# Routed attention and a SoLU feed-forward on one core: 1024-wide steps on h, one-hot rows placed by DMA, a first pair in halves, and a new order

## The chip, the cores and the metric

The kernel runs on one core of one Trainium2 chip. The metric is the device time of an execution in microseconds (us). TensorE is called PE (PEld: its weight loads), VectorE DVE, ScalarE ACT, GpSimd POOL, and SyncE, whose queue issues nearly all transfers, SP.

## The reference

For batch 4, 8 heads, 768 tokens and 64 dimensions, each token's q and k is assigned to the nearest of 16 centroids of its head, and attention runs only between tokens of the same cluster. The result, as 3072 rows of 512, goes through a feed-forward layer with a SoLU and a layer norm.

```python
q_assign = argmax(einsum(q_n, c_n)); k_assign = argmax(einsum(k_n, c_n))
mask = q_assign[:, :, :, None] == k_assign[:, :, None, :]
scores = where(mask, q @ k.T / sqrt(D), -1e9)
x = (softmax(scores) @ v).transpose(0, 2, 1, 3).reshape(B * S, H * D)
h = x @ w_in                        # 3072 x 1024
e = exp(h - max(h))
solu = h * e / sum(e)
ln = (solu - mean(solu)) / sqrt(var(solu) + 1e-6) * g_ln
out = ln @ w_out
```

## The kernel before, in words

**Attention.** Work goes by pairs of heads, 16 pairs over four batches. A pair's q and k arrive as raw tiles by DMA and are turned to dimensions by tokens (`xt`): in batch 0 by PE transposes into PSUM and a copy (L303, L311, L313), later by a DVE transpose of 32x32 blocks (L326). The result is cast to bf16 into `qbig` and `kbig`, one of six slots (L332 to L336, on POOL or ACT). `clusters` (L346) multiplies by the centroids; DVE turns the scores back (L353), takes the maximum of 16 (L358), compares (L362, the one-hot), and turns that again (L368, `oht`). `place` (L375) copies the one-hot rows into the same tile as the vectors: rows 64 to 95 for the even head, rows 0 to 31 for the odd one, whose vector lies in rows 64 to 127. That takes eight copies of 32x192 words a pair, on POOL or DVE. Half of the 32 rows belong to the other head, and `blank` (L379) clears those of k. A score matmul (L458) over vector and one-hot rows together so gives q.k plus a large constant for equal clusters, which the exponential (L463) turns into the mask. One bank is 128x512 scores; the score ring has three banks, the ring of exponentials `e` nine. Six matmuls of 65 columns (L475) then give the values with the sum, and `normalise` (L487, L498) divides.

**Feed-forward.** There are 24 blocks f of 128 tokens. x is turned by a DMA transpose (L506); `f_h` (L539) makes h in two halves of 512, each in a bank of a ring of three; `f_max` (L546) takes a maximum of each half and `f_neg` (L550) joins them; `f_exp` (L557) and `f_u` (L563) run on each half; u is turned by a DMA transpose (L568); statistics (L574, L578) give the scale `alpha` on POOL (L584 to L590); `f_y` (L600) and `f_scale` (L606 ACT, L608 DVE) end the block, and `f_out` (L613) writes it. The last x and the last two u are turned by PE instead (L515, L525). w_in is cast by POOL (L408), w_out is scaled and centred by DVE (L425 to L437).

**The order.** Every step is put into a list by `add` with an engine, a cost, a key, and what it needs. `Weave.run` (L76) goes through the list as a planner would, with those costs, and issues each engine's instructions in the order that results. Steps that could start at about the same time go by key; FEED, PAIR and KIND shift the keys, and AWAY names the steps that go to another engine than their usual one. The order is therefore fixed when the program is built, and each engine, SP's queue too, works through its own list strictly in turn.

Of the kernel before, what the change touches and what calls it, by code (L numbers as in the profile page):

```python
# [21 lines left out]
class Weave:  # L22

    FEED_KINDS = "tx ptx tu ptu hm h ng ex u bn ag al y sc ou".split()
    PAIR_KINDS = "ld tp xa xt ca lv cv cl tb mx oh ot pl bl".split()
    FEED = [-1, 2, 2.5, 4.5, 5, 4, 6.5, 11, 18, 7.5, 8, 12.5, 7.5, 21, 10, 15.5, 16.5, 10.5,
        4.5, 7.5, 1.5, 0.5, 2.5, -0.5]
    PAIR = [-27, 0, 1.5, -6, -9, -4.5, 0, -3, 19.5, -7.5, 1.5, -3, 21, 13.5, 21, 19.5]  # L30
    KIND = {'cv': -23.5, 'wi': -36.0, 'tb': -12.0, 'ca': 16.0, 'xa': 20.0, 'N': -1.0, 'tp':
        38.0, 'lg': 36.5, 'lo': -4.0, 'pl': -3.0, 'bl': 11.5, 'z': 35.5, 'xt': -1.0, 'lv': 1.5,
        'ce': -1.0, 'oh': -1.0, 'su': 0.5, 'ld': 5.0, 'li': 4.0, 'ot': -1.0, 'cl': 0.5, 'mx':
        0.5}
    AWAY = {}
    AWAY.update(dict.fromkeys("""
        ca0.0.1.0 ca0.0.1.1 ca0.1.0.0 ca1.1.1.0 ca1.2.1.0 ca1.3.0.1 ca2.1.0.0 ca2.1.0.1
        ca2.2.0.1 ca2.3.0.0 ca3.3.0.1 xa0.0.0 xa0.2.0 xa0.2.1 xt0.2.0 xt0.2.1 xt0.3.1
    """.split(), "ACT"))
    AWAY.update(dict.fromkeys("""  # L40
        bl3.2 bl3.3 pl0.0.0.1.0 pl0.0.0.1.1 pl0.0.1.1.0 pl3.0.0.1.1 pl3.2.0.0.0 pl3.2.0.1.0
        pl3.3.0.1.0 sc15 sc17 sc22
    """.split(), "DVE"))
    AWAY.update(dict.fromkeys("""
        bl0.0 ca0.0.0.0 ca0.0.0.1 pl0.0.0.0.0 pl0.0.0.0.1 pl0.0.1.0.0 pl0.0.1.0.1
        pl0.2.1.0.1 pl0.2.1.1.1
# [4 lines left out]
    AHEAD = 2  # L51
# [5 lines left out]
    def add(self, name, eng, cost, key, fn, needs=(), after=(), take=None, give=None, move=0.0,  # L57
            bulk=False, lag=(0.5, 0.6)):
        assert name not in self.by, name
        key += self.later(name)  # L60
        self.by[name] = len(self.ops)
        self.ops.append(dict(name=name, eng=eng, cost=cost, key=key, fn=fn, needs=list(needs),
                             after=list(after), take=take, give=give, move=move,
                             bulk=bulk, lag=lag))

    def later(self, name):

        kind, rest = re.fullmatch(r"([A-Za-z]+)(.*)", name).groups()
        if kind in self.FEED_KINDS:
            return self.FEED[int(rest.split(".")[0])]  # L70
        if kind in self.PAIR_KINDS:
            b, p = rest.split(".")[:2]
            return self.PAIR[4 * int(b) + int(p)] + self.KIND.get(kind, 0)
        return self.KIND.get(kind, 0)

    def run(self):  # L76
# [67 lines left out]
        for i in order:  # L144
            ops[i]["fn"]()
# [3 lines left out]
def kernel(  # L149
# [20 lines left out]
    HALF = S // 2  # L170
    d_model = H * D
# [22 lines left out]
    ps_h = ctx.enter_context(tc.tile_pool(name="ps_h", bufs=3, space=bass.MemoryType.PSUM))  # L194
# [7 lines left out]
    def on(name, engine):  # L202
        return wv.AWAY.get(name, engine)

    R = 6
    qbig = [big.tile([P, 2, S], BF16, name=f"qbig{i}") for i in range(R)]
    kbig = [big.tile([P, 2, S], BF16, name=f"kbig{i}") for i in range(R)]
    v1 = [big.tile([P, 2, n_t, VS], BF16, name=f"v1_{i}") for i in range(R)]

    def slot(b, p):  # L210
        return (b * n_pair + p) % R

    def behind(b, p, what):
# [6 lines left out]
        return [f"{what}{n}.{k}" for n in ns for k in range(n_k if what == "S" else 2)]  # L220

    SRC, DST = (q, k), (qbig, kbig)

    def rows(h):
        return slice(0, D) if h % 2 == 0 else slice(D, P)

    def hot_rows(hh):
        return slice(D, D + NB) if hh == 0 else slice(0, NB)

    def used(h):  # L230
        return slice(0, D + NC_) if h % 2 == 0 else slice(0, P)

    n_first = 2
    UNITS, GROUPS = [], []
    for b in range(B):
        if b < B - 1:
            for p in range(n_pair):
                a, c = 2 * p, 2 * p + 1  # L240
                if p < n_pair - 1:
                    hs = [[(h, s2) for s2 in range(n_t // 2)] for h in (a, c)]
                else:
                    hs = [[(a, s2), (c, s2)] for s2 in range(n_t // 2)]
                for grp in hs:
                    GROUPS.append([])
                    for h, s2 in grp:
                        GROUPS[-1].append(len(UNITS))
                        UNITS.append((b, ((h, 2 * s2), (h, 2 * s2 + 1))))
        else:  # L250
            for h in range(2 * n_first):
                GROUPS.append([])
                for s2 in range(n_t // 2):
                    GROUPS[-1].append(len(UNITS))
                    UNITS.append((b, ((h, 2 * s2), (h, 2 * s2 + 1))))
            for su in range(n_t):
                for h in range(2 * n_first, H, 2):
                    if h % 4 == 0 or h == 2 * n_first:
                        GROUPS.append([])
                    GROUPS[-1].append(len(UNITS))  # L260
                    UNITS.append((b, ((h, su), (h + 1, su))))
    n_units = len(UNITS)
    n_k = 3
    group_of = {n: g for g, ns in enumerate(GROUPS) for n in ns}
    where = {(b, h, su): n for n, (b, subs) in enumerate(UNITS) for h, su in subs}

    def same_head(n):
        return UNITS[n][1][0][0] == UNITS[n][1][1][0]

    def spot(n, j, kt):  # L270

        if same_head(n):
            return kt // 2, (kt % 2) * 2 * P + j * P
        m = j * n_t + kt
        return m // 4, (m % 4) * P

    def first_of(b, p):
        return 2 * min(n for (b2, h, su), n in where.items() if b2 == b and h // 2 == p)
# [9 lines left out]

    def tokens(b, p, i):
        return raws[b, p, i][:].rearrange("p j c -> p (j c)").rearrange("p (t e) -> p t e", t=n_t)  # L290

    def load_tokens(b, p, i, hh, eng):
        if hh == 0:
            raws[b, p, i] = ld.tile([P, n_j, NB], F32, name="raw")
        eng.dma_start(out=tokens(b, p, i)[:, :, hh * D:(hh + 1) * D],
                      in_=SRC[i][b, 2 * p + hh].rearrange("(p t) d -> p t d" if i else
                                                          "(t p) d -> p t d", p=P))

    def turn_tokens(b, p, i, hf):

        tps[b, p, i, hf] = ps_h.tile([P, HALF], F32, name="tps", tag="hps")
        for t in range(n_t // 2):
            nc.tensor.transpose(tps[b, p, i, hf][:, t * P:(t + 1) * P],  # L303
                                tokens(b, p, i)[:, hf * (n_t // 2) + t, :], ident_f[:])

    def keep_tokens(b, p, i, hf, e):
        if hf == 0:
            xts[b, p, i] = xtp.tile([P, S], F32, name="xt")
        dst, src = xts[b, p, i][:, hf * HALF:(hf + 1) * HALF], tps[b, p, i, hf][:]
# [18 lines left out]
    def cast(b, p, i, hh, on_act=False):  # L328
        xt, h = xts[b, p, i], 2 * p + hh
        r, dst = rows(h), DST[i][slot(b, p)]  # L330
        if on_act:
            nc.scalar.activation(dst[r, hh, :], xt[r], Act.Copy, scale=inv_C if i else 1.0)  # L332
        elif i == 0:
            nc.gpsimd.tensor_copy(dst[r, hh, :], xt[r])  # L334
        else:
            nc.gpsimd.tensor_scalar(dst[r, hh, :], xt[r], scalar1=inv_C, scalar2=1.0,  # L336
                                    op0=Alu.mult, op1=Alu.mult)

    n_a = n_j // 2 * 2

    def clusters(b, p):

        csc = ps_m.tile([P, HALF], F32, name="csc", tag="m")
        for c in range(4):
            i, hf = divmod(c, 2)
            nc.tensor.matmul(csc[c * NB:(c + 1) * NB, :], c_bd[:, p, :],  # L346
                             xts[b, p, i][:, hf * HALF:(hf + 1) * HALF],
                             tile_position=(0, c * NB))
        asg[b, p, "csc"] = csc

    def turn_back(b, p):
        asg[b, p, "cst"] = pr.tile([P, n_a, NC_], F32, name="cst")
        nc.vector.transpose(asg[b, p, "cst"][:].rearrange("p a c -> p (a c)"),  # L353
                            asg[b, p, "csc"][:])

    def assign_max(b, p):
        asg[b, p, "mx"] = pr.tile([P, n_a], F32, name="mx")
        nc.vector.reduce_max(asg[b, p, "mx"][:], asg[b, p, "cst"][:], axis=AX)  # L358

    def assign_hot(b, p):  # L360
        asg[b, p, "oh"] = pr.tile([P, n_a, NC_], BF16, name="oh")
        nc.vector.tensor_tensor(asg[b, p, "oh"][:], asg[b, p, "cst"][:],  # L362
                                asg[b, p, "mx"][:].unsqueeze(2).to_broadcast([P, n_a, NC_]),
                                op=Alu.is_ge)

    def assign_turn(b, p):
        asg[b, p, "oht"] = pr.tile([P, HALF], BF16, name="oht")
# [585 lines left out]
```

## Time and profile before

| | |
|---|---|
| Median of 3 runs | 245.14 us (244.53 to 246.28) |
| Span of the profiled execution | 241.7 us |
| Instructions | 6735 |
| PE first score matmul | at 14.11 us |
| PE first feed-forward matmul | at 59.58 us |
| PE last matmul ends | at about 237.9 us |
| POOL copies of one-hot rows (L375) | 107, 39.5 us together |
| Exponentials of scores (L463) | 288, 149.5 us together |

The page gives one profiled execution: each engine's busy time, the chain of work that ended last, and groups of instructions by line with their count, busy time and the mean of one in nanoseconds. An answer by stretches gives the engines' busy times between two points of the span. The timeline lists instructions in order of time: start, length, engine, line. The runs' median lies 3.4 us above the profiled span.

### The profile page before, as it was taken

The numbers are of one execution on the slowest core, as the hardware profiler recorded it, in microseconds if no ns is written. First come the engines' busy times: TensorE is split into PE (matmuls) and PEld (weight loads), VectorE is DVE, ScalarE is ACT, GpSimd is POOL, SyncE is SP. The second block draws the span as 40 slices with busy tenths as digits, with TensorE's granted clock in tenths as the row PEclk, the third lists the DMA queues.
The fourth block names the chain that finished last, engine by engine and source line by source line (L and its number), as shares of the span: only waits on it lengthen the run. The fifth ranks groups of instructions, "written<-read, shape, count | busy, mean of one in ns | idle before, by whom it ended". The sixth has DMA issues, their size and how long they took to land.

```text
span 241.7 us, 6735 instructions
## 1 busy us (share of the span) xinstructions
PE 221.2 (92%) x2384; PEld 148.5 (61%) x2384; DVE 207.1 (86%) x427; ACT 205.4 (85%) x428; POOL 141.2 (58%) x304
## 2 busy tenths in 40 slices
PE   0969999999999999899699999999989999999983
PEld 0656675666656667666377677567657676747441
DVE  4367599999999998999699999988969779999991
ACT  2559998999788999999699999988989998969561
POOL 4973687997083485998757738888812510310331
PEclk9979999999999999999999999999999999999999
DMA  7999889797489799999799999783533444657422
GB/s 200 269 280 263 180 305 237 150 152 171 84 177 193 152 190 201 205 146 193 112 173 209 209 155 161 169 238 87 66 75 59 69 110 110 69 152 151 92 87 87
DMA packets 133217, 38.61 MB, mean 160 GB/s; under 512 B 124472, under 2 KB 128576, under 8 KB 133184
## 3 DMA queue, kind: packets, MB, share of 16 engines
q1 hardware_dynamic: 131616, 37.80, 76.9%
q10 hardware_dynamic: 1568, 0.39, 0.7%
q8 instruction: 18, 0.29, 0.5%
q14 instruction: 15, 0.12, 0.2%
HBM read 23.11 MB, written 6.29 MB: 122 GB/s over the span
## 4 chain that ended last, share of the span: by engine, by line
PE 65%; DVE 10%; DMA 7%; POOL 6%; ACT 5%; issue 5%; ACTq 0%; DVEq 0%; SPq 0%; POOLq 0%
PE sps L458 18%; PE yps L600 14%; PE hps L539 14%; PE ops L475 11%; PE csc L346 4%; ACT e L463 4%; DMA uT<-u 4%; PE tps L303 2%; DMA xT<-x 2%; DVE w_out_c L437 2%; POOL kbig L336 1%; DVE hm L546 1%; POOL qbig L334 1%; DVE qbig L375 1%; ACT e_sb L557 1%
## 5 line engine op out<-in xcount | busy, mean ns | idle before, releaser
L463 ACT ACTIVATE e<-sps 128x512 bf16<-128x512 f32 x288 | 149.5, 625 | 13.5 <-PE sps L458 12.6
L458 PE MATMUL sps<-qbig,kbig 80*128 80x256 bf16 (+3 forms) x648 | 102.2, 265 | 5.2 <-POOL qbig L375 2.1
L458 PEld LDWEIGHTS <-kbig 80*128 80x128 bf16 (+1 forms) x648 | 58.9, 122 | 24.3 <-issue 9.7
L475 PEld LDWEIGHTS <-e 128*128 128x128 bf16 x1152 | 57.5, 98 | 20.5 <-issue 3.8
L475 PE MATMUL ops<-v,e 128*128 128x65 bf16 x1152 | 65.7, 194 | 0.9 <-DVE x L498 0.6
L539 PE MATMUL hps<-w_in_sb,xT 128*128 128x512 bf16 x192 | 53.2, 379 | 2.8 <-DMA xT<-x 2.1
L600 PE MATMUL yps<-w_out_c,uT 128*128 128x512 bf16 x184 | 45.4, 379 | 1.6 <-DMA uT<-u 1.4
L557 ACT ACTIVATE e_sb<-hps,nmax 128x512 bf16<-128x512 f32 x48 | 32.9, 699 | 3.0 <-DVE nmax L550 2.9
L546 DVE TENSOR_REDUCE hm<-hps 128x1 f32<-128x512 f32 x48 | 31.9, 676 | 3.3 <-PE hps L539 2.9
L563 DVE TENSOR_TENSOR u<-e_sb,hps 128x512 bf16<-128x512 bf16 x48 | 31.6, 678 | 2.6 <-ACT e_sb L557 2.5
L375 POOL COPY kbig<-oht 32x192 f32<-32x192 f32 x57 | 20.8, 364 | 20.9 <-DVE oht L368 18.6
L574 DVE BATCH_NORM_STATS2 bs<-u 128x6 f32<-128x512 bf16 x48 | 31.6, 678 | 0.0
L600 PEld LDWEIGHTS <-uT 128*128 128x128 bf16 x192 | 17.8, 98 | 18.3 <-DMA uT<-u 1.8
L587 POOL TENSOR_SCALAR esq<-es,mv 128x1 f32<-128x1 f32 x24 | 8.2, 340 | 34.6 <-DVE mv L578 33.3
L334 POOL CAST qbig<-xt 64x768 bf16<-64x768 f32 x25 | 21.5, 859 | 6.8 <-ACT xt L311 5.9
L336 POOL TENSOR_SCALAR kbig<-xt 64x768 bf16<-64x768 f32 x28 | 23.3, 834 | 2.8 <-DVE xt L313 1.3
L539 PEld LDWEIGHTS <-xT 128*128 128x128 bf16 x192 | 17.1, 97 | 11.7 <-DMA xT<-x 2.3
L326 DVE STREAM_TRANSPOSE xt<-raw 128x768 f32<-128x768 f32 x24 | 22.1, 951 | 0.1
L375 POOL COPY qbig<-oht 32x192 f32<-32x192 f32 x50 | 18.7, 375 | 2.6
L498 DVE TENSOR_TENSOR x<-ops,den 128x384 bf16<-128x384 f32 (+1 forms) x37 | 18.6, 504 | 1.3
L389 POOL CAST v<-vf 128x384 bf16<-128x384 f32 x32 | 15.7, 514 | 6.3 <-DMA vf<-in_v_dram 3.3
L606 ACT ACTIVATE y<-yps,alpha 128x512 f32<-128x512 f32 x20 | 13.9, 694 | 5.5 <-POOL alpha L590 2.8
(74 smaller groups left out, 188.8 us busy)
## 6 DMA issues: line engine op xcount, KB each, us to landing
vf<-in_v_dram SPq DMA_DIRECT2D x16, 384.0 KB, 4.2
out_dram<-y SPq DMA_DIRECT2D x24, 256.0 KB, 2.4
raw<-in_q_dram SPq DMA_DIRECT2D x48, 96.0 KB, 3.5
raw<-in_k_dram SPq DMA_DIRECT2D x48, 96.0 KB, 2.7
w_st<-in_moe_w_in_dram SPq DMA_DIRECT2D x4, 512.0 KB, 5.6
w_g<-in_moe_w_out_dram SPq DMA_DIRECT2D x4, 512.0 KB, 7.2
raw<-in_q_dram SPq DMA_DIRECT2D x7, 192.0 KB, 4.2
raw<-in_k_dram SPq DMA_DIRECT2D x7, 192.0 KB, 4.4
```

The lines of the kernel that those rows point to most:

```text
L334: nc.gpsimd.tensor_copy(dst[r, hh, :], xt[r])
L336: nc.gpsimd.tensor_scalar(dst[r, hh, :], xt[r], scalar1=inv_C, scalar2=1.0, op0=Alu.mult, op1=Alu.mult)
L375: (nc.vector if e == "DVE" else nc.gpsimd).tensor_copy(dst, src)
L458: nc.tensor.matmul(sps_[n, k][:, c0:c0 + w], kbig[z][u, h % 2, keys], qbig[z][u, h % 2, q0:q0 + w])
L463: nc.scalar.activation(es[n, k][:], sps_[n, k][:], Act.Exp, scale=exp_scale, bias=-exp_scale)
L475: nc.tensor.matmul(opss[g][:, s, :VW], es[n, k][:, c0:c0 + P], v1[slot(b, h // 2)][:, h % 2, kt, :VW], start=(kt == 0), stop=(kt == n_t - 1))
L539: nc.tensor.matmul(ff[f, "h", f2][:], xTs[f][:, dc, :], w_in_sb[:, dc, f2 * FF2:(f2 + 1) * FF2], start=(dc == 0), stop=(dc == n_dc - 1))
L546: nc.vector.tensor_reduce(ff[f, "hm"][:, f2:f2 + 1], ff[f, "h", f2][:], axis=AX, op=Alu.max)
L557: nc.scalar.activation(ff[f, "e"][:, f2, :], ff[f, "h", f2][:], Act.Exp, bias=ff[f, "nmax"][:], accum_out=ff[f, "esum"][:, f2:f2 + 1])
L563: nc.vector.tensor_tensor(ff[f, "u"][:, f2, :], ff[f, "e"][:, f2, :], ff[f, "h", f2][:], op=Alu.mult)
L574: nc.vector.bn_stats(ff[f, "bs"][:, f2, :], ff[f, "u"][:, f2, :])
L600: nc.tensor.matmul(ff[f, "y"][:], ff[f, "uT"][:, fc, :], w_out_c[:, fc, :], start=(fc == 0), stop=(fc == n_fc - 1))
```

## The change

- The maximum of h, the exponential and the product each run once over both halves (1024 wide). h lies in a fixed region of three banks, and a block uses banks 0 and 1 or banks 1 and 2 in turn. The joining of two maxima goes; the sum of the exponentials is one number, whose scaled epsilon is formed in a step of its own.
- q and k of both heads lie in one tile `qk`; each head's vector is in rows 0 to 63 and its one-hot rows below, in rows 64 to 95. A pair is placed by four DMAs on SP's queue, which write both heads' copy at once (L437), instead of eight copies. The score matmuls of the odd head run over 96 rows, not 128.
- From the third pair on, the one-hot is made by a subtraction on POOL and a compare with zero on DVE or POOL.
- The first pair is loaded, turned, assigned and placed in two halves, by POOL copies; its score banks are 384 wide (24 of them, for 18 of 512).
- In batch 0 q is read with six tokens in a row for each partition, as k was, and the output rows are written to suit.
- Casts of q, k, v and w_in, the last copies and the scalings of y may now run on DVE too. FEED, PAIR, KIND, AWAY and many costs are new, and with them the whole order. By the built programs DVE has 18 casts of q and k (two of them of half size), 8 of v, 2 of w_in and 10 scalings of y (3 before); ACT has 15 casts (11 before) and 14 scalings (21 before).

The diff, cut to its core:

```diff
-    qbig = [big.tile([P, 2, S], BF16, name=f"qbig{i}") for i in range(R)]
-    kbig = [big.tile([P, 2, S], BF16, name=f"kbig{i}") for i in range(R)]
+    qk = [big.tile([P, 2, 2, S], BF16, name=f"qk{i}") for i in range(R)]
+    hreg = ps_h.tile([P, 3, FF2], F32, name="hreg")
...
+        else:
+            subs = [(h, 3 * s + j) for j in range(3)]
+            banks = [[(h, kt, 3 * s, 3 * P, 0)] for kt in range(n_t)]
...
+        dst = qk[slot(b, p)][:D, hh, i, cols]
...
+    def assign_less(b, p, hf):
+        nc.gpsimd.tensor_tensor(by_group(b, p, hf, "cst"), by_group(b, p, hf, "cst"),
+                                spread_max(b, p, hf), op=Alu.subtract)
...
+        if less:
+            VEC[e].tensor_scalar(asg[b, p, hf, "oh"][:, :n], asg[b, p, hf, "cst"][:, :n],
+                                 scalar1=0.0, scalar2=None, op0=Alu.is_ge)
...
-        dst = DST[i][slot(b, p)][hot_rows(hh), hh, hf * HALF:(hf + 1) * HALF].bitcast(F32)
-        (nc.vector if e == "DVE" else nc.gpsimd).tensor_copy(dst, src)
+        dst = qk[slot(b, p)][D:D + NB, :, i, lo:lo + n]
+        src = asg[b, p, hf, "oht"][r, :n]
+        if e == "SP":
+            nc.sync.dma_start(out=dst, in_=src.unsqueeze(1).to_broadcast([NB, 2, n]))
...
+    def at(f, f2):
+        return (f2, f2) if f % 2 == 0 else (1 - f2, 2 - f2)
+    def pair_of(f):
+        return hreg[:, 0:2, :] if f % 2 == 0 else hreg[:, 1:3, :]
...
-        nc.vector.tensor_reduce(ff[f, "hm"][:, f2:f2 + 1], ff[f, "h", f2][:], axis=AX, op=Alu.max)
+        nc.vector.tensor_reduce(ff[f, "nmax"][:], pair_of(f), axis=AXY, op=Alu.max, negate=True)
...
-        nc.scalar.activation(ff[f, "e"][:, f2, :], ff[f, "h", f2][:], Act.Exp,
-                             bias=ff[f, "nmax"][:], accum_out=ff[f, "esum"][:, f2:f2 + 1])
+        nc.scalar.activation(ff[f, "e"][:], pair_of(f), Act.Exp, bias=ff[f, "nmax"][:],
+                             accum_out=ff[f, "esum"][:])
...
-        nc.vector.tensor_tensor(ff[f, "u"][:, f2, :], ff[f, "e"][:, f2, :], ff[f, "h", f2][:],
-                                op=Alu.mult)
+        nc.vector.tensor_tensor(ff[f, "u"][:], ff[f, "e"][:], pair_of(f), op=Alu.mult)
...
-    for i in range(2):
-        for hh in range(2):
-            load_tokens(0, 0, i, hh, (nc.scalar, nc.sync)[hh])
+    for hf in range(2):
+        for i in range(2):
+            for hh in range(2):
+                load_tokens(0, 0, i, hh, 3 * hf, 3 * hf + 3, (nc.scalar, nc.sync)[hh])
...
+            less = idx >= 2
...
+                e = ("DVE", "POOL")[j % 2] if half else "SP"
...
+                    was = f - 1 if f2 else f - 2
+                    if was >= 0:
+                        nd.append(f"u{was}")
```

More of the change, by code (lines that the diff above doesn't have):

```diff
@@ new lines, with wide @@
+    n_units = len(UNITS)
+    group_of = {n: g for g, ns in enumerate(GROUPS) for n in ns}
+    where = {(u["b"], h, su): n for n, u in enumerate(UNITS) for h, su in u["subs"]}
+    spots = {}
+    for n, u in enumerate(UNITS):
+        for j, bank in enumerate(u["banks"]):
+            for h, kt, s0, w, c0 in bank:
+                for s in range(w // P):
+                    spots[n, h, s0 + s, kt] = (j, c0 + s * P)
+    def wide(n, j):
+        return sum(w for _, _, _, w, _ in UNITS[n]["banks"][j])
@@ L213, in behind, with first_of @@
+    time_of, spent = {}, 0
+    for n, j in BANKS:
+        time_of[n, j] = spent / (1.5 * FF2) * 2
+        spent += wide(n, j) / 2
+    t_of = [min(time_of[n, j] for j in range(len(UNITS[n]["banks"]))) for n in range(n_units)]
+    t_to = [max(time_of[n, j] for j in range(len(UNITS[n]["banks"]))) for n in range(n_units)]
+    t_all = spent / (1.5 * FF2) * 2
+    def first_of(b, p):
+        return min(t_of[n] for (b2, h, su), n in where.items() if b2 == b and h // 2 == p)
     def behind(b, p, what):
@@ L219, in behind @@
         ns = sorted({where[b0, 2 * p0 + hh, su] for hh in range(2) for su in range(n_t)})
[L220 to L278, printed above, removed]
+        return [f"{what}{n}.{j}" for n in ns
+                for j in range(len(UNITS[n]["banks" if what == "S" else "subs"]))]
     pairs = [(b, p) for b in range(B) for p in range(n_pair)]
@@ L377, in blank, with turn_back, by_group @@
-    def blank(b, p, e):
-        (nc.vector if e == "DVE" else nc.gpsimd).memset(
-            kbig[slot(b, p)][:NC_, 1, :].bitcast(F32), 0.0)
+        asg[b, p, hf, "csc"] = csc
+        asg[b, p, hf, "n"] = n
+    def turn_back(b, p, hf):
+        n = asg[b, p, hf, "n"]
+        asg[b, p, hf, "cst"] = pr.tile([P, HALF], F32, name="cst")
+        nc.vector.transpose(asg[b, p, hf, "cst"][:, :n], asg[b, p, hf, "csc"][:, :n])
+    def by_group(b, p, hf, what):
+        n = asg[b, p, hf, "n"]
+        return asg[b, p, hf, what][:, :n].rearrange("p (a c) -> p a c", c=NC_)
@@ L634 @@
     nc.vector.memset(c_bd[:], 0.0)
-    for i in range(2):
-        nc.vector.memset(DST[i][0][NB:D, 1, :].bitcast(F32), 0.0)
     nc.gpsimd.memset(v1[0][:, :, :, D:], 1.0)
@@ new lines @@
+            nd += [f"V{n0}.{j}" for j, (h, su) in enumerate(UNITS[n0]["subs"])
+                   if any(spots[n0, h, su, kt][0] == k0 for kt in range(n_t))]
+        add(f"E{n}.{k}", "ACT", 0.05 + wide(n, k) / 1200, t0 - 1,
+            (lambda e, n=n, k=k: expo(n, k)), nd, ["E{}.{}".format(*BANKS[i - 1])] if i else [])
+    prev = None
+    for g, ns in enumerate(GROUPS):
+        for n in ns:
+            u = UNITS[n]
+            b = u["b"]
+            for j, (h, su) in enumerate(u["subs"]):
+                nd = sorted({f"E{n}.{spots[n, h, su, kt][0]}" for kt in range(n_t)})
+                nd.append(f"cv{b}.{h // 2}.{h % 2}")
+                if 0 < b * n_pair + h // 2 < R:
+                    nd.append(f"z{b * n_pair + h // 2}")
+                if n == ns[0] and j == 0 and g:
+                    nd.append(f"N{g - 1}")
+                add(f"V{n}.{j}", "PE", 0.193, t_to[n] - 1 + j + 0.5,
+                    (lambda e, n=n, j=j: values(n, j)), nd, [prev] if prev else [])
+                prev = f"V{n}.{j}"
+        nd = [prev]
+        if b >= 2:
+            nd += [f"tx{(b - 2) * n_t + s2}" for s2 in range(n_t)]
+        m = sum(len(UNITS[n]["subs"]) for n in ns)
+        add(f"N{g}", "DVE", 0.29 + 0.067 * m, t_to[ns[-1]] - 2,
+            (lambda e, g=g: normalise(g)), nd)
```

721 lines of the change are left out of this document (393 added, 328 removed), and 6 rows, old and new, of the table KIND.

## The prediction

> **What bounds the kernel now.** I read the page's busy table and chain first, then the same busy times cut into stretches, then the rows behind the stretches that lose time.
>
> ```profile
> PE 221.2 (92%) x2384; PEld 148.5 (61%) x2384; DVE 207.1 (86%) x427; ACT 205.4 (85%) x428; POOL 141.2 (58%) x304
> ...
> PE 65%; DVE 10%; DMA 7%; POOL 6%; ACT 5%; issue 5%; ACTq 0%; DVEq 0%; SPq 0%; POOLq 0%
> ```
>
> TensorE (PE) carries 65% of the chain; three engines are near full. But a busy PE counts pipelined matmuls at full length. Their real price is the pitch in the chain's rows:
>
> ```profile
> 26.24 1.14 PE ops L475 x36
> ...
> 134.79 0.45 PE sps L458 x4
> ...
> 137.28 0.78 PE csc L346 x8
> ...
> 162.81 1.73 PE yps L600 x8
> ```
>
> So 0.032 us for a value product, 0.112 for a score of 256 columns (0.057 for 128), 0.195 for a csc (eight records of two passes are four matmuls), 0.217 for an FFN matmul. With the counts: 504 and 144 scores 64.5, 1152 values 36.5, 384 FFN 83.1, 64 csc at 0.195 12.5, 69 transposes 9.1, the mean 1.0: 206.7 us. The span is 241.7, so PE lacks work for 35 us. Where:
>
> ```profile
> 6.00:14.00 8.00, 5.97 (x30) 3.82 (x29) 4.08 (x10) 3.12 (x5) 6.25 (x17) 1.00 1.15 270
> 40.00:50.00 10.00, 9.42 (x132) 6.74 (x129) 9.61 (x18) 9.44 (x20) 9.37 (x18) 1.00 0.85 145
> 90.00:105.00 15.00, 13.85 (x156) 9.96 (x158) 14.04 (x27) 14.42 (x32) 11.24 (x27) 1.00 0.99 192
> 105.00:120.00 15.00, 12.88 (x150) 8.13 (x142) 12.83 (x24) 13.79 (x27) 13.00 (x28) 1.00 0.97 153
> 120.00:135.00 15.00, 15.00 (x169) 10.86 (x163) 13.75 (x27) 14.21 (x31) 10.36 (x23) 1.00 1.01 185
> 225.00:241.70 16.70, 12.16 (x69) 5.52 (x68) 11.16 (x25) 6.57 (x14) 5.16 (x14) 1.00 0.28 94
> ```
>
> Columns: stretch, length, busy PE, PEld, DVE, ACT, POOL, clock, DMA share, GB/s. Nothing runs on PE for scores until 14.11 (9.4 of the 35). From there to the first FFN matmul at 59.58 PE works 36.4 of 45.5: DVE and ACT are full, ACT sets it (9.1). From 59.58 to PE's end at 237.9, 165.6 of 178.3 is work (12.7 lost), and 3.8 follow PE. In 120:135 PE has no gap, and 16 FFN, 46 score and 84 value matmuls make 15 us of real work: there only less PE work would help, and the change removes none. In 90:120 PE loses 4.1, and POOL is at 13.00 of 15.
>
> ```profile
> 109.59 0.74 POOL L375 COPY kbig<-oht 32x192 f32<-32x192 f32 x2
> ...
> 113.51 0.72 POOL L375 COPY kbig<-oht 32x192 f32<-32x192 f32 x2
> ```
>
> ```profile
> 117.91 0.60 PE L539 MATMUL hps<-w_in_sb,xT 128*128 128x512 bf16 x2 [2.10 <-DMA xT<-x]
> ```
>
> These are POOL's placing copies in the timeline, eight in a row for each pair, and the row in which PE waits longest (2.10, for a transposed x). From 98.5 to 111.9 the chain runs through POOL row by row and then into that transfer.
>
> **The change, part by part.** The counts are those of the two instruction orders. PE: 24 scores 384 wide replace 36 of 256, the rest is equal; zero.
>
> *1024 wide.* DVE: two maxima start to start take 1.28 (67.89 to 69.17), the joining one 0.08 more. A normalisation of 384 elements takes 558 ns and one of 256 424, so an element costs 1.05 ns; the 1024-wide maximum is 676 + 512 x 1.05 = 1.21, pitch 1.14 (bounds 0.68 and 1.28). Saved: 0.2 a block. The product: 1.14 for 1.2 to 1.28, 0.1. ACT: a pair of exponentials with its two accumulator reads takes 1.33 (62.48 to 63.81); ACT's 64x768 cast at 846 against its 384 copy at 534 gives 0.81 ns an element, so one wide is 0.67 + 0.42 = 1.09 (bounds 0.90, 1.33). Saved 0.24. Over 24 blocks: 7 us of DVE, 6 of ACT, none of it PE's. Lost: the halves no longer overlap; maximum, exponential and product in a row take 3.4 where the tail now shows 2.9. The middle bank of h is in every block, so a block's second half waits for the product before: a loop of 0.87 + 3.4 and three handovers, 4.6 us, inside the 6.9 that a block gets (165 us / 24). Cover: that slack; without it up to 0.5 each.
>
> *Placing by DMA.* POOL loses 107 copies of 364 to 375 ns (39.5 us), DVE 21 (7.9). POOL gains 14 subtractions (128x384, between its cast of that shape, 0.51, and its 1024 cast, 1.03; I take 0.8: 11 us) and 9 compares (4). With 23 casts and 8 value casts sent to ACT and DVE (24 us) it falls from 141 to about 105. SP gains 60 issues; an output issue takes 0.47 (111.05), so 28 us on a queue that issues for about 142 now (96 loads x 0.57, 45 transposes x 1.25, the rest 31). Each stands behind its turned one-hot, and loads, transposes and outputs behind it. A transfer lands in 2.2 (centroids) to 5.8 (the xT of 112.07); eight POOL copies take 3.1. I take zero net, covered by the pairs prepared ahead; if that cover is gone, up to 3 a pair.
>
> *DVE's new work.* 18 casts of q and k (two of them halves), 8 of v, 2 of w_in, 7 more y, 5 light compares instead of 15 full ones. A y takes 0.75. A 768 cast lies between the 0.25 of a small copy and the 0.95 of the 768 transpose; nearest is the tensor_scalar of 512 in SBUF, 0.478, so about 0.6. Added 18 to 26, removed 25 (7 wide, 7.9 placing, 6.7 compares, 2.5 product, 0.8 memsets). DVE stays at 200 to 208.
>
> These new casts meet POOL at a place that the trace shows:
>
> ```profile
> 33.62 3.44 DVE L375 COPY qbig<-oht 32x192 f32<-32x192 f32 x4
> ```
>
> ```profile
> 33.67 1.03 POOL L408 CAST w_in_sb<-w_st 128x1024 bf16<-128x1024 f32 x1
> 34.77 0.83 POOL L334 CAST qbig<-xt 64x768 bf16<-64x768 f32 x1
> ```
>
> Four DVE copies of 0.25 each (the line's minimum is 247 ns, its maximum 1200) took 3.44 while POOL cast: 0.6 lost on each. The Trainium skill (SBUF — State Buffer, Who interferes with whom) says why: copies, casts and tensor_scalar from SBUF to SBUF take a port pair that the two engines share, and whoever is first holds it for the whole instruction. This row agrees, and the rule speaks against moving casts to DVE. By the rows alone: 33 such operations x 0.6 x the 0.43 of the span that POOL is busy = 8.5 us, at worst all on DVE.
>
> *First pair by halves.* Now: transposes end at 8.64, csc 10.71, four DVE steps of 0.55 to 0.6, placing, scores at 14.11. After: c_bd is ready at 6.6 as now; nine transposes at 0.213 end at 8.0; half csc 1.04; four half steps, each shorter by 192 x 1.05 ns, 1.55; a copy stands between (0.5); four POOL placings 1.4: scores at 12.6. **-1.5** (bounds 0, and -2.2 without the copy).
>
> *New order.* 74 banks stand ahead of the first FFN matmul, not 80: at ACT's pitch 0.51, -3.1. The first 24 are 384 wide (0.41 by 0.81 ns an element; bounds 0.38, 0.51): 24 x 0.41 for 18 x 0.51, +0.7 to +0.9. ACT also does three casts more and one copy less there, +1.7. **-0.5.** But 3.0 us of PE work (41.1 ahead now, 38.1 then) move behind: **+3.0.** In 90:120 the pacing POOL is relieved: of 4.1 I take back **-3.5** (bounds 0, and -8 with all small gaps). Tail: now 13.0 us hold 11.5 of PE work behind the last values (48 FFN matmuls, 20 transposes). After it is 76 and 20, 17.6, and a walk through the loop of 4.6 finds half-blocks ready just as the outputs between them end: **-0.8**.
>
> Sum: -1.5 - 0.5 + 3.0 - 3.5 - 0.8 = -3.3; span 238.4. The median of the runs, 245.1, is 3.4 over the profiled span of 241.7; that stays: 241.8 us.
>
> **Rivals.**
> 1. *All waits behind the first FFN matmul shrink* (12.7 to 4), since POOL, ACT and their handovers have room. 57.6 + 168.5 + 4 + 3.8 = 233.9, so 237.3. For: 120:225 shows PE without gaps. Against: DVE is as full as before.
> 2. *DVE remains as full, and the shared place with POOL eats the rest.* DVE 208 + 8.5 = 216.5, and ahead of the first block about 48 us of it for 47 now: start and tail gains stay, the others go: -1.5 + 3.0 - 0.8 = +0.7, 245.8. For: four copies at 33.62 lost 2.4. Against: POOL has 36 us less to hold the place with. This is what the rule of the Trainium skill quoted above (SBUF — State Buffer, Who interferes with whom) would make of it.
> 3. *Slower: placing holds SP's queue.* One late one-hot keeps xT and uT behind it. The price of one is the row at 117.91, where PE waited 2.1 for an xT that took 5.79. SP issues 170 of 240 us and has waits besides (it already waits 18.7 for y and 24.7 for u and its statistics). Twelve pairs are placed while FFN blocks run; if four or more hold a transpose that PE is waiting for, 4 x 2.1 outweighs the sum: 241.8 + 8 = 249.8. For: DMA share 0.97 to 1.03 in 75:150. Against: pairs are prepared ahead. It ends slower than before from the third such wait on (3.3 + 2.5 for the percent).
> 4. *The loop of the middle bank paces*: wherever blocks follow closer than 4.6, PE stops; 0.5 in half of the 24 is 6, 247.8. That also stands for the case that the 1024-wide forms give nothing on PE's path.
>
> **How the numbers follow.** Forecast 0.42 (its own range 240 to 244), rival 1 0.24, rival 2 0.16, rival 3 0.13, rival 4 0.05. A measurement of this kernel can tell about 1% from no change: faster is below 242.7, slower above 247.6. Faster: 0.30 of the forecast and 0.24 = 0.54; same: 0.12 of it and 0.12 of rival 2 = 0.24; slower: 0.04, 0.13, 0.05 = 0.22. The range leaves out the far ends of rivals 1 and 3: 236.5 to 248.
>
> **What would show it.** First scores at 12 to 13; first FFN matmul near 57.6; the wide maximum near 1.2, the exponential near 1.1; POOL near 105 and DVE 200 to 208 us busy; in 90:120 no POOL wait on the chain. Wrong if PE sits idle for xT, uT or the placed rows (rival 3), for the product on the middle bank (4), or if DVE copies of SBUF data stretch to over 1 us beside POOL (2).

## The result

The changed kernel takes 286.99 us (median of 4 runs, 285.18 to 288.05), the kernel before beside it 244.83 (244.27 to 246.28): 1.178 times as long, 95% interval 1.169 to 1.188. The forecast was 241.8 us, the range 236.5 to 248.0. The profiled execution spans 283.2 us. Runs more than 1.5% above the fastest of their kernel are left out of the times and ratios that follow, though not of the times that the expectations quote.

The page of the changed kernel (busy times, chain, and the rows of h: L610 its matmuls, L616, L621 and L626 the wide maximum, exponential and product):

```profile
PE 230.1 (81%) x2349; PEld 148.8 (53%) x2380; DVE 208.8 (74%) x361; ACT 201.2 (71%) x384; POOL 101.7 (36%) x191
...
PE 39%; DVE 25%; DMA 11%; issue 8%; ACT 8%; SPq 4%; POOL 4%; DVEq 0%; ACTq 0%; POOLq 0%
...
L610 PE MATMUL hreg<-w_in_sb,xT 128*128 128x512 bf16 x174 | 49.4, 378 | 23.9 <-DVE nmax L616 8.9
...
L626 DVE TENSOR_TENSOR u<-e_sb,hreg 128x1024 bf16<-128x1024 bf16 x24 | 29.1, 1215 | 20.6 <-ACT e_sb L621 10.8
L621 ACT ACTIVATE e_sb<-hreg,nmax 128x1024 bf16<-128x1024 f32 x24 | 26.9, 1121 | 19.1 <-PE hreg L610 9.6
...
L616 DVE TENSOR_REDUCE nmax<-hreg 128x1 f32<-128x1024 f32 x24 | 29.1, 1211 | 2.7 <-PE hreg L610 2.6
```

The sizes are as forecast: wide maximum 1.211 us (1.21), exponential 1.121 (1.09), POOL 101.7 us busy (105), DVE 208.8 (200 to 208). But no engine is full any more, and PE's share of the chain has fallen from 65% to 39%, DVE's risen from 10% to 25%. PE sat idle for 23.9 us just before h matmuls. The same by stretches (columns as in the prediction):

```profile
6.00:14.00 8.00, 6.36 (x34) 2.92 (x32) 3.88 (x11) 1.87 (x4) 3.19 (x7) 1.00 0.98 246
40.00:50.00 10.00, 8.92 (x101) 6.85 (x101) 6.27 (x13) 6.59 (x14) 3.49 (x5) 0.66 0.60 191
90.00:105.00 15.00, 12.55 (x128) 8.12 (x133) 12.59 (x21) 12.35 (x24) 8.48 (x11) 1.00 0.76 149
105.00:120.00 15.00, 12.95 (x153) 9.41 (x148) 12.83 (x21) 12.21 (x24) 8.13 (x12) 1.00 1.01 152
120.00:135.00 15.00, 12.38 (x139) 7.94 (x140) 14.22 (x24) 13.02 (x25) 6.85 (x12) 1.00 0.93 176
270.00:283.20 13.20, 8.30 (x49) 3.95 (x48) 6.71 (x11) 5.01 (x8) 2.04 (x5) 0.96 0.21 83
```

POOL is relieved in 90:120 (16.6 us for 24.2), and PE loses more there all the same (by its busy time 4.5 us of 30, for 3.3). The first scores come at 15.65 us (14.11 before), the first feed-forward matmul at 66.76 (59.58), and from there to the end it takes 216.4 us for 182.1: 1.5, 5.6 and 34.3 of the 41.5 us.

```profile
15.65 0.49 PE L514 MATMUL sps<-qk 80*128 80x384 bf16 x2
...
66.76 1.02 PE L610 MATMUL hreg<-w_in_sb,xT 128*128 128x512 bf16 x3 [0.53 <-DVE w_out_c L500]
```

The view of PE's waits names what is new:

```profile
PE hreg L610 <- DVE nmax L616: 8.9, 10, 1.3
PE hreg L610 <- ACT e_sb L621: 6.3, 8, 1.8
PE hreg L610 <- DVE u L626: 5.5, 5, 1.6
```

(Columns: us in all, times, longest.) An h matmul should never wait for a maximum or an exponential. The first half of a block goes into a bank that the block before does not use, the second half into the middle bank, which comes free only with the product. One such wait in the timeline:

```profile
206.37 1.03 PE L610 MATMUL hreg<-w_in_sb,xT 128*128 128x512 bf16 x3
...
207.44 1.23 DVE L616 TENSOR_REDUCE nmax<-hreg 128x1 f32<-128x1024 f32 x1 [1.07 <-PE hreg L610]
...
208.71 0.59 PE L610 MATMUL hreg<-w_in_sb,xT 128*128 128x512 bf16 x2 [1.31 <-DVE nmax L616]
```

A block's h ends, its maximum runs, and PE stands for 1.31 us until that has ended, although its next matmul writes the third bank and the maximum reads the other two. The built program says the same: the third h matmul of block 3, into bank 2, waits for the semaphore of the maximum of block 2, which reads banks 0 and 1. A tile is a named buffer, and the program's waits between engines follow from which step uses which tile. The three banks were three tiles; now they are one tile, `hreg`, and the waits are made for the whole of it. So each step on one bank waits for every step listed earlier that used another, the turned tokens of the start too. The planner's `needs` know nothing of these waits, so it lists steps in an order in which they bind. That is the main theory, "one tile". Its rivals: placing by DMA, the 1024-wide steps themselves, POOL's slower steps, and the new order.

### The profile page after: what moved, and what is told of

Its sections match the earlier page's. It is cut to its first block, busy times and chain, and to the rows that moved or that the text cites. A ratio compares the mean times of both kernels' runs of the same rounds, so it can differ in the third digit from the quotient of the medians.

```text
span 283.2 us, 6579 instructions
## 1 busy us (share of the span) xinstructions
PE 230.1 (81%) x2349; PEld 148.8 (53%) x2380; DVE 208.8 (74%) x361; ACT 201.2 (71%) x384; POOL 101.7 (36%) x191
## 4 chain that ended last, share of the span: by engine, by line
PE 39%; DVE 25%; DMA 11%; issue 8%; ACT 8%; SPq 4%; POOL 4%; DVEq 0%; ACTq 0%; POOLq 0%
PE sps L514 10%; PE hreg L610 9%; PE yps L666 7%; PE ops L537 6%; DVE nmax L616 5%; DMA raw<-in_k_dram 4%; DVE u L626 4%; ACT e L520 3%; DVE bs L636 3%; DMA qk<-oht 3%; PE hreg L343 3%; DVE xt L366 3%; PE csc L386 2%; SPq L358 2%; SPq L437 2%
## 5 line engine op out<-in xcount | busy, mean ns | idle before, releaser
L520 ACT ACTIVATE e<-sps 128x512 bf16<-128x512 f32 (+1 forms) x294 | 149.0, 613 | 29.2 <-PE sps L514 28.4
L514 PE MATMUL sps<-qk 80*128 80x256 bf16 (+5 forms) x636 | 105.2, 269 | 6.4 <-ACT e L520 2.8
L514 PEld LDWEIGHTS <-qk 96*128 96x128 bf16 (+1 forms) x636 | 57.7, 123 | 26.0 <-issue 15.0
L610 PE MATMUL hreg<-w_in_sb,xT 128*128 128x512 bf16 x174 | 49.4, 378 | 23.9 <-DVE nmax L616 8.9
L626 DVE TENSOR_TENSOR u<-e_sb,hreg 128x1024 bf16<-128x1024 bf16 x24 | 29.1, 1215 | 20.6 <-ACT e_sb L621 10.8
L621 ACT ACTIVATE e_sb<-hreg,nmax 128x1024 bf16<-128x1024 f32 x24 | 26.9, 1121 | 19.1 <-PE hreg L610 9.6
L610 PEld LDWEIGHTS <-xT 128*128 128x128 bf16 x192 | 18.2, 97 | 39.6 <-issue 28.6
L616 DVE TENSOR_REDUCE nmax<-hreg 128x1 f32<-128x1024 f32 x24 | 29.1, 1211 | 2.7 <-PE hreg L610 2.6
L375 POOL CAST qk<-xt 64x768 bf16<-64x768 f32 (+1 forms) x20 | 15.8, 788 | 26.2 <-DVE xt L366 13.7
L411 POOL TENSOR_TENSOR cst<-cst,mx 128x384 f32<-128x384 f32 x14 | 12.4, 886 | 13.7 <-DVE mx L408 13.7
L386 PE MATMUL csc<-xt,c_bd 128*32 128x384 f32 (+1 forms) x136 | 16.5, 501 | 0.0
```

The costliest lines, as they stand in the source:

```text
L386: nc.tensor.matmul(csc[c * NB:(c + 1) * NB, :n], c_bd[:, p, :], xts[b, p, i][:, lo + part * n:lo + (part + 1) * n], tile_position=(0, c * NB))
L514: nc.tensor.matmul(sps_[n, k][:, c0:c0 + w], qk[z][r, h % 2, 1, keys], qk[z][r, h % 2, 0, s0 * P:s0 * P + w])
L520: nc.scalar.activation(es[n, k][:, :w], sps_[n, k][:, :w], Act.Exp, scale=exp_scale, bias=-exp_scale)
L610: nc.tensor.matmul(hreg[:, at(f, f2)[1], :], xTs[f][:, dc, :], w_in_sb[:, dc, f2 * FF2:(f2 + 1) * FF2], start=(dc == 0), stop=(dc == n_dc ...
L616: nc.vector.tensor_reduce(ff[f, "nmax"][:], pair_of(f), axis=AXY, op=Alu.max, negate=True)
L621: nc.scalar.activation(ff[f, "e"][:], pair_of(f), Act.Exp, bias=ff[f, "nmax"][:], accum_out=ff[f, "esum"][:])
```

## The experiments: one tile

**e1**: the kernel before, its order kept; only its tiles become banks of one.

```diff
+hreg = ps_h.tile([P, 3, 512], F32, name="hreg")    # ps_h: bufs=1
-ff[f, "h", f2] = ps_h.tile([P, FF2], F32, name="hps", tag="hps")
+ff[f, "h", f2] = hbank()        # the banks of hreg in turn; so for tps, mps, ype
```

> The kernel before, same order, all steps 512 wide; only its three separate one-bank PSUM tiles (turned tokens, mean, h, last y) become three banks of one tile. One-tile theory (the program waits on the whole three-bank tile, so that each matmul into one bank waits for the steps that still read the other two): 265 to 300 us, with waits of PE for the maximum, exponential and product of the block before that the kernel before does not have. Every rival (placing by DMA; 1024-wide steps holding the middle bank; slower POOL and DVE steps; the new order) leaves it at 244 to 247.

Measured: 288.93 us (ratio 1.178, 1.169 to 1.186), the kernel before 244.69. The one tile alone, with nothing else of the change, costs the kernel before 44.2 us. Its PE waits:

```profile
PE hreg L546 <- DVE u L570: 19.8, 20, 2.9
...
PE hreg L546 <- ACT e_sb L564: 5.5, 6, 1.2
PE hreg L546 <- DVE hm L553: 5.2, 10, 0.8
```

These three are 30.5 us; the kernel before has 0.2 us of them in all (one wait, for a product). PE's mean clock, as a share of full speed, is 0.964 here and 0.993 before, which can be up to 8.6 us more (287.1 x 0.036 - 241.7 x 0.007).

**e2** and **e3**: the changed kernel, its order kept, with maximum, exponential and product 512 wide, two at a time; in e2 also three tiles, in e3 the one.

```diff
-nc.scalar.activation(ff[f, "e"][:], pair_of(f), Act.Exp, ...)
+for f2 in range(n_ff2):    # so for the maximum and the product
+    nc.scalar.activation(ff[f, "e"][:, at(f, f2)[0], :], bank_of(f, f2), Act.Exp, ...)
-hreg = ps_h.tile([P, 3, FF2], F32, name="hreg")    # e2 alone
+hreg = [ps_h.tile([P, FF2], F32, name=f"hreg{i}") for i in range(3)]
```

> The changed kernel with the same order, its three h banks as three separate tiles; for that the maximum, exponential and product are 512 wide again, two at a time, back to back. Placing by DMA, halves at the start, casts and order stay. One-tile theory: 238 to 252 us. Wide-step theory (a 1024-wide step holds the middle bank too long): about the same, 240 to 255. Placing theory, slower-POOL theory, order theory: 270 or more, since all of that stays.

> The changed kernel with the same order and one three-bank tile, but maximum, exponential and product 512 wide, two at a time. One-tile theory: 280 to 295 us, since the waits stay and the narrow steps cost a little more. Wide-step theory: 240 to 255.

Measured: e2 264.5 us (ratio 1.082, 1.076 to 1.088), e3 295.3 (two runs, 293.9 and 296.8). With all else equal the one tile costs 30.8 us in the changed order; the wide steps win back about 8.3 (295.3 against 287.0): PE's waits for maximum, exponential and product are 26.2 us in e3 and 20.7 in the changed kernel. In e2 the waits are gone. From 60 us on all that is left for h on PE is:

```profile
PE hreg L610 <- DMA xT<-x: 2.0, 2, 1.3
...
PE hreg L610 <- DVE u L632: 0.6, 1, 0.6
```

But e2 is not at 238 to 252. One tile explains most of the loss, and 20 us have another cause.

**e5**: the changed kernel; the planner is told of the waits.

```diff
-was = f - 1 if f2 else f - 2
+was = f - 1                       # h waits for the product of the block before
-n2 = [...] + ring_h[-3:-2]
+n2 = [...] + ring_h[-1:]
```

> The changed kernel, one tile and 1024-wide steps as they are, but the planner is told that a block's first h matmul comes behind the product of the block before, and each turn of tokens behind the copy before it, so that the order fits the waits that the program has. One-tile theory: 245 to 262 us, the serial chain of h matmuls 1.7, maximum 1.2, exponential 1.1 and product 1.2 is some 6 us a block against the 6.9 that a block has, so most of the loss is the order that did not know of the waits. Placing, slower-POOL and wide-step theories: 275 or more.

Measured: 313.2 us (ratio 1.280, 1.272 to 1.287). A miss. With the old shifts of the keys the planner now puts blocks late: the last matmul of attention ends at 219.3 us, and what follows is bare blocks, one after the other:

```profile
225.00:240.00 15.00, 9.18 (x40) 3.58 (x39) 10.49 (x13) 4.64 (x8) 2.45 (x7) 1.00 0.41 96
```

Sixteen matmuls are a block, so 40 in 15 us are 6.0 us a block, as much as the serial chain that I had estimated; but PE's waits from 225 us on are for uT (13.4 us) as well as for the product (11.9), and it runs with no attention beside it. That a told planner could hide the chain is not shown.

## The experiments: the other 20 us

**e6, e7, e67**: e2 in its very order. e6: all rows placed by POOL copies. e7: the one-hot by DVE's one compare as before, no subtraction. e67: both.

```diff
-nc.sync.dma_start(out=dst, in_=src.unsqueeze(1).to_broadcast([NB, 2, n]))              # e6
+nc.gpsimd.tensor_copy(dst.bitcast(F32), src.bitcast(F32).unsqueeze(1).to_broadcast(...))
-nc.gpsimd.tensor_tensor(cst, cst, mx, op=Alu.subtract)                                  # e7
-VEC[e].tensor_scalar(oh, cst, scalar1=0.0, scalar2=None, op0=Alu.is_ge)
+nc.vector.tensor_tensor(oh, cst, mx, op=Alu.is_ge)
```

> The three-tile kernel (264.5 us) in its very order, but the one-hot rows of all pairs but the first are placed by POOL copies at the same points of the order instead of 60 DMAs on SP's queue. What is asked is where the 20 us come from that separate tiles leave open. Placing theory (the DMAs hold SP's queue and delay xT, uT and the loads): 248 to 257 us. Compare theory (POOL's compare takes 1.2 us where the planner has 0.46, so that one-hot rows come late): 264 to 272, POOL being busier by 60 copies. Order theory (the new order, planned with prices that do not hold): 261 to 270.

> The three-tile kernel in its very order, but the one-hot rows are found by one compare on DVE as in the kernel before (0.6 us), and POOL's subtraction and compare (0.89 and 1.2 us) are gone. Compare theory: 250 to 258 us. Placing theory: 262 to 267. Order theory: 260 to 267.

> Both at once: rows placed by POOL copies and found by DVE's one compare, three tiles, the new order. If placing and compare together are the 20 us: 244 to 250. Order theory: 258 to 266, the order alone keeps most of the loss.

Measured: 259.86, 264.01 and 253.78 us (ratios 1.068, 1.086, 1.046, each to within 0.012; the kernel before beside them spread from 241.6 to 246.2). Against e2's ratio of 1.082 they give 3.5 and -0.9 us alone, neither clear of noise, and 8.9 together, which is. Why both together give more than the sum is not shown. What the placing does on PE is seen in its waits, first in e2, then in e6:

```profile
PE yps L674 <- DMA uT<-u: 5.4, 3, 3.3
...
PE sps L514 <- DMA qk<-oht: 0.5, 1, 0.5
```

```profile
PE yps L675 <- DMA uT<-u: 1.5, 1, 1.5
```

With DMAs PE hardly waits for the placed rows (0.5 us), but for turned u: 5.4 us in e2 and 8.0 in e7, 1.5 in e6 and e67. In e2's longest such wait (3.33 us, to 106.69) the last product ends at 98.48, and SP's queue, busy with loads that stand behind three placings, starts the transpose at 102.41.

**e8, e9, e14**: the kernel before with placing by DMA alone (both heads' vectors move to rows 0 to 63 for it). e8 keeps its order, e9 has the planner told, e14 is e8 with the DMAs issued from POOL's queue.

```diff
-nc.gpsimd.tensor_copy(dst, src)                 # eight a pair, 32x192
+nc.sync.dma_start(out=DST[i][slot(b, p)][D:D + NB, :, cols],    # four a pair; e14: nc.gpsimd
+                  in_=asg[b, p, "oht"][r, :].unsqueeze(1).to_broadcast([NB, 2, HALF]))
```

> The kernel before in its very order and with separate tiles; only both heads' vectors lie in rows 0 to 63 and the one-hot rows of all pairs but the first are placed below them by 60 DMAs of both heads at once, at the points where the first of the two copies stood. Placing theory: 254 to 265 us. Compare and order theories: 242 to 248, POOL and DVE are relieved of 120 copies of 0.4 us and little waits for the DMAs.

> As e8 (278.0 us), but the planner is told of the 60 DMAs (a start on SP's queue of 0.5 us, landing some 2 us later), so that the order is made for them. If e8's 34 us are an order that left no time for a DMA's landing: 246 to 258 us. If placing by DMA costs in itself, through SP's queue or the DMA engines, whatever the order: 263 or more.

> As e8 (278.0 us; the kernel before with the one-hot rows placed by 60 DMAs), but POOL issues the DMAs and SP's queue holds what it held before. If SP's queue is what costs (0.6 us a start, and xT, uT and loads behind each that waits for its rows): 245 to 258 us. If the landing of some 2 us is what costs: 268 to 282.

Measured: 276.70 (ratio 1.142, 1.128 to 1.156), 273.19 (1.119, 1.107 to 1.132) and 271.85 us (1.120, 1.112 to 1.128). So placing by DMA costs the kernel before 29 to 34 us, whichever queue issues it and whether or not the order knows of it; that SP's queue alone is at fault is refuted for this order. (A transfer lands 3.0 to 3.2 us after its issue in e14, 2.0 in e8, so e14 does not tell starts from landings.) PE's waits in e8:

```profile
PE sps L469 <- DMA qbig<-oht: 15.5, 4, 5.7
...
PE yps L611 <- DMA uT<-u: 3.3, 4, 1.7
```

The timelines of one pair show what e8 adds. First the kernel before, then e8: the turned one-hot (`oht`), the placing, the scores that wait for it.

```profile
31.39 0.56 DVE L368 STREAM_TRANSPOSE oht<-oh 128x384 bf16<-128x384 bf16 x1
...
31.99 0.57 DVE L375 COPY kbig<-oht 32x192 f32<-32x192 f32 x2
...
33.62 3.44 DVE L375 COPY qbig<-oht 32x192 f32<-32x192 f32 x4
...
35.38 0.87 PE L458 MATMUL sps<-qbig,kbig 80*128 80x256 bf16 x4
```

```profile
30.35 0.57 DVE L369 STREAM_TRANSPOSE oht<-oh 128x384 bf16<-128x384 bf16 x1
...
32.51 1.24 SPq L385 DMA_DIRECT2D kbig<-oht  x2
...
35.07 0.59 SPq L385 DMA_DIRECT2D qbig<-oht  x1
...
36.33 0.59 SPq L385 DMA_DIRECT2D qbig<-oht  x1
...
37.66 1.01 PE L469 MATMUL sps<-qbig,kbig 80*128 80x256 bf16 x4 [2.74 <-DMA qbig<-oht]
```

From the end of `oht` to the pair's first scores it is 3.4 us before and 6.7 in e8: 1.6 until SP starts the first of four DMAs of 0.6 us, 3.8 until it starts the fourth, with loads between them, and 1.3 from there.

Pairs differ in this. Taken for each pair from the trace, in the program's order, the time in the kernel before is 1.6 to 4.2 us for eight of the fifteen pairs behind the first, and 5.3 to 20.5 for the other seven. So about half the pairs were prepared ahead. The four waits of e8 for placed rows (15.5 us) all stand before pairs that had 1.6 to 3.8. In e9, where the planner knows of the DMAs, the time is 6.7 us or more for every pair behind the first, and PE waits for uT instead (9.1 us in six waits); why that order costs as much is not shown.

Part of the price can be PE's clock. In e9 PE waits 1.92 us for a uT, after a thin stretch (timeline, then the stretches; the clock is the third number from the right, 1.00 being full speed):

```profile
79.00 2.76 PE L611 MATMUL yps<-w_out_c,uT 128*128 128x512 bf16 x8 [1.92 <-DMA uT<-u]
```

```profile
76.00:78.00 2.00, 1.08 (x17) 0.75 (x14) 1.89 (x4) 2.00 (x7) 0.40 (x2) 1.00 0.58 83
78.00:80.00 2.00, 1.00 (x5) 0.53 (x6) 1.97 (x5) 0.91 (x2) 0.00 (x0) 0.97 0.93 148
80.00:82.00 2.00, 2.00 (x12) 0.90 (x10) 0.82 (x1) 0.14 (x1) 0.89 (x2) 0.50 1.04 234
82.00:84.00 2.00, 2.00 (x16) 1.02 (x14) 0.35 (x1) 0.61 (x2) 1.31 (x3) 0.67 1.08 239
```

PE then runs at half clock and loses 1.7 us more (2 x 0.50 + 2 x 0.33). Over e9's whole span the mean clock is 0.934, at most 18.0 us lost (272.7 x 0.066); in the kernel before it is 0.993, 1.7 us; in the changed kernel 0.980, 5.7. The loss is well under that bound: a run of e9 at 0.974 took 270.66 us, only 3.8 less than the profiled one.

**e15**: the kernel before in its order, with the changed compare alone.

```diff
-nc.vector.tensor_tensor(oh, cst, mx, op=Alu.is_ge)
+nc.gpsimd.tensor_tensor(cst, cst, mx, op=Alu.subtract)      # from the third pair on
+(nc.gpsimd if 5 <= idx <= 13 else nc.vector).tensor_scalar(oh, cst, scalar1=0.0,
+                                                           scalar2=None, op0=Alu.is_ge)
```

> The kernel before in its very order, with the change's compare alone: from the third pair on POOL subtracts the maximum (0.9 us) and the compare with zero is POOL's (1.2 us) for nine pairs and DVE's (0.4 us) for five. If one-hot rows that come some 1.5 us later are on the path: 249 to 262 us. If the slack before the scores covers it: 243 to 248.

Measured: 257.03 us for 242.36 (ratio 1.061, 1.053 to 1.070). 14.7 us for 14 pairs are 1.05 us a pair, near what the steps add to the way to the rows (1.5 us for nine pairs, some 0.7 for five, by the rows below: 1.2 on average). That fits rows that come late and count nearly one for one. But the steps also put 22.4 us more on POOL, and this run does not separate the two. The steps in the changed kernel, on POOL and, for five pairs, on DVE:

```profile
L411 POOL TENSOR_TENSOR cst<-cst,mx 128x384 f32<-128x384 f32 x14 | 12.4, 886 | 13.7 <-DVE mx L408 13.7
...
L418 POOL TENSOR_SCALAR oh<-cst 128x384 bf16<-128x384 f32 x9 | 11.1, 1228 | 0.7
```

```profile
L418 DVE TENSOR_SCALAR oh<-cst 128x384 bf16<-128x384 f32 x5 | 2.0, 404 | 0.0
```

**e10, e11**: e2 and e67 with new shifts and engines in the planner's tables, found for the measured durations; nothing else changes. **e12, e13**: the same work with h in two separate two-bank tiles and 1024-wide steps, the score ring cut to two banks, tables again new; e12 places by DMA, e13 by POOL with the one compare.

```diff
-hreg = ps_h.tile([P, 3, FF2], F32, name="hreg")                                 # e12, e13
+hreg = [ps_h.tile([P, 2, FF2], F32, name=f"hreg{i}") for i in range(2)]         # block f: f % 2
-ps_s = ... tc.tile_pool(name="ps_s", bufs=3, ...)
+ps_s = ... tc.tile_pool(name="ps_s", bufs=2, ...)
```

> The three-tile kernel (264.5 us; DMA placing, POOL's subtraction, halves at the start all stay), with new offsets and engines in the planner's tables, found for the durations that the traces show (two 512-wide steps 1.36, 1.32 and 1.26 us, POOL's compare 1.2, DVE's casts 0.64 to 0.78). Order theory (the 20 us beside the one tile are an order made for prices that do not hold): 247 to 257 us. Placing or compare theory (they cost in any order): 259 to 266.

> As the last, but rows placed by POOL copies and found by DVE's one compare (its counterpart in the old tables took 253.8 us). Order theory: 247 to 254. If this is below the DMA-placing run beside it by more than 3 us, placing and compare cost also where the order knows of them.

> The whole change with 1024-wide maximum, exponential and product, but h in two separate two-bank tiles (even and odd blocks) instead of one of three banks, the scores' ring cut from three banks to two to make room, and the order made for it by the planner. One-tile theory: the waits between blocks are gone, 244 to 256 us. Wide-step theory (1024-wide steps cost by holding h's banks), or the scores' shorter ring: 260 or more.

> Like e12 (272.2 us; 1024-wide steps on two separate two-bank tiles, scores' ring of two, order made for it), with rows placed by POOL copies and found by DVE's one compare. Its neighbour with 512-wide steps on three tiles, e11, took 263.6. If wide steps and the shorter ring cost nothing: 256 to 266 us, e12 being slow by its placing. If the shorter ring or the wide steps cost: 268 or more.

Measured: e10 268.88, e11 263.57, e12 272.07, e13 257.96 us (ratios 1.102, 1.082, 1.114, 1.063, each to within 0.013). The new tables are worse than the old (264.5 and 253.8), so that measured durations in the planner are enough is refuted. At tables of the same making, placing by DMA with POOL's compare costs 2 and 5% (e10 over e11, e12 over e13). Wide steps on separate tiles, shorter ring included, cost nothing: e13 stands 1.9% below e11, though with an order of its own.

**e16, e17, e18**: e67 in its order. e16 gives the casts that the new tables put on DVE back to POOL, e17 eight scalings of y back to ACT, e18 both.

```diff
+e = "POOL" if e == "DVE" and (b, p) != (0, 0) else e       # e16, in cast(); cast_v likewise
-if e == "ACT":
+if e == "ACT" or f not in (15, 17):                        # e17, in f_scale()
```

> As e67 (three tiles, POOL placing, one compare: 253.8 us), in its very order, with the casts of q, k and v that the new tables put on DVE (pairs after the first) back on POOL. If DVE's load is the last 9 us: 246 to 251 us. If it is the order: 251 to 258, POOL being later.

> As e67, with eight of the ten scalings of y that the new tables put on DVE back on ACT (0.75 us of DVE each, 6 us). DVE theory: 247 to 252. Order theory: 252 to 257.

> Both of these. DVE theory: 242 to 249, the kernel before or a little better. Order theory: 251 to 258.

Measured: 248.60 us (ratio 1.027, 1.022 to 1.032), 255.54 (1.056) and 250.89 (1.035), the kernel before at 241.62. The casts on DVE cost about 2% (e16 against e67 at 1.046, e18 against e17), the scalings nothing: back on ACT they make it about 1% slower. The stretch 60:150 of e67, then of e16:

```profile
60.00:150.00 90.00, 82.05 (x906) 56.31 (x918) 85.86 (x166) 78.25 (x164) 47.36 (x88) 1.00 0.93 168
```

```profile
60.00:150.00 90.00, 85.48 (x959) 58.31 (x957) 81.59 (x160) 80.48 (x169) 55.04 (x101) 1.00 0.96 175
```

DVE falls from 85.9 to 81.6 of 90 us, and PE's work rises from 82.1 to 85.5. The last 2.7%, 6.6 us, stay open: the new order, the start by halves and what else of the change is left were not told apart. No version tried beats the kernel before.

In sum, from 244.8 us: placing and compare about 9, casts on DVE about 4.5, order and the rest about 6.5 (together 19.8, e2), the one tile +30.8 (e3), the wide steps -8.3: 287.1, measured 287.0.

## Why the prediction was wrong

**The step that failed** is the one on the middle bank: "a block's second half waits for the product before: a loop of 0.87 + 3.4 and three handovers, 4.6 us, inside the 6.9 that a block gets", "Cover: that slack; without it up to 0.5 each". I took the waits from the data, where only the middle bank is shared. The program waits for the whole three-bank tile, and no term of the sum was for that: 30.8 us in this order, 44.2 in the other. The cause stood in the diff (`ps_h` from three tiles to one) and in the waits of the built program. The Trainium skill (PSUM — Partial Sum Buffer, PSUM bank collisions raise a hardware error) asks for a guard by bank; the kernels with three tiles run with just that, so the added waits are wider than the chip needs. Rival 4 was the nearest, at 6 us and a chance of 0.05.

**Placing, "I take zero net, covered by the pairs prepared ahead"**: wrong. The cover is there for about half the pairs, and where it is short the rows come late: 29 to 34 us alone in the old order, in the changed one 3.5 with POOL's compare left (about the noise) and, by the ratios 1.086 and 1.046, about 10 without it. Rival 3 had the sign and nearly the size for the changed order (8 us), and its wait is seen there: PE waits 5.4 to 8.0 us for uT with DMAs and 1.5 without. In the old order the rows themselves come late (e8), and clearing SP's queue of the DMAs does not help (e14).

**The compare**, "9 compares (4)" on POOL: 11.1 us, 1228 ns each; and I had priced it as POOL's load alone, when it lies on the way to the scores too; that fits the 14.7 us of e15, which does not tell the two apart.

**DVE's new work** was sized well (casts 644 and 734 ns for 0.6; 208.8 us busy), but "DVE stays at 200 to 208" did not make it free: the casts cost about 2% (e16). The sign of rival 2 appeared twice: a cast of q took 1.10 us, and one of v 2.47, from 34.22, with POOL at work beside it, where the shortest of its form took 0.32. That is far from the 41.5 us.

**First pair by halves, -1.5**: right in kind, hidden. With three tiles the first scores come at 12.99 us (forecast 12.6, before 14.11); with the one tile at 15.65, since the transposes wait for copies out of other banks (PE's waits for such copies sum to 3.6 us).

**New order and POOL's relief, -0.5, +3.0, -3.5**: the first feed-forward matmul was due at 57.6 and comes at 60.9 with three tiles, 66.8 as changed; POOL was relieved and PE gained nothing by it. **The tail, -0.8**: not seen, the one tile paces it. (Of the working, 120:135 holds 32 FFN matmuls, 16 of each kind; its 15 us are right with 32. And 2.10 is PE's longest wait only behind the first scores, which waited 2.13.)

**1024 wide**: durations right; the gain of about 8.3 us where the chain of a block binds was not foreseen, as I saw none of it on PE's path.

## What to carry to other kernels

When buffers are merged into one tile, read the waits of the built program before counting on banks: steps on separate parts may be tied together, and an order planned without these waits runs into them again and again. In a tightly ordered kernel ask of each step on the way to the bounding engine's input how many microseconds lie between its result and the first use, each time that it runs; here delays of 1 to 3 us a pair hurt where that time was under 4 us. And price a wait on PE with the slow clock that can follow it.

## What was not expected of the hardware

PE's clock fell to half around pauses of some 2 us, but not after every one, and once without one. After 1.92 us (e9, above) it was 0.50 to 0.67 for 4 us; in the kernel before a pause of 2.13 us ahead of the first scores was followed by 0.72 over 14:20, while one of 2.10 us before 117.91 left it at 1.00. In e9 it also fell over 66:68, where the longest wait of PE since 60 us was 0.29. First the kernel before, then e9:

```profile
14.00:20.00 6.00, 5.89 (x56) 4.12 (x55) 3.02 (x7) 5.03 (x9) 5.54 (x12) 0.72 1.11 287
```

```profile
64.00:66.00 2.00, 1.73 (x22) 1.15 (x19) 1.97 (x5) 2.00 (x5) 0.00 (x0) 1.00 0.81 142
66.00:68.00 2.00, 1.85 (x9) 0.65 (x6) 1.28 (x3) 0.66 (x2) 0.00 (x0) 0.56 0.72 201
```

So the pause alone does not decide it; what does is not shown. The Trainium skill (TensorE: Matmul & The Clock Gate, HAM oscillation — how this bites in real kernels) speaks of idle gaps beyond about 3.4 us; the pauses here are shorter, and in e9 a thin stretch of PE work lay around the pause.

POOL's compare of 128x384 f32 with a constant took 1228 ns, more than its subtraction of two such operands (886), and three times DVE's 404.
